# A chunk's decay table made on the chip, eight early load buffers, idle matmuls in the opening, a new order

## The chip, the cores and the metric

One core of one Trainium2 chip runs the whole program. The metric is device time in microseconds (us); the kernel before takes 593.6 us, the median of three runs (593.54 to 593.75). The engines are TensorE (PE; PEld is its weight load), VectorE (DVE), ScalarE (ACT), GpSimd (POOL) and SyncE (SP), which here issues all the DMAs.

## The reference, cut to what matters

```python
gamma = 1.0 - 2.0 ** (-5.0 - np.arange(H))               # retention: B=2, H=8, S=768, D=64
for t in range(S):
    state = gamma * state + k[:, :, t] (outer) v[:, :, t]
    y[:, :, t] = scale * q[:, :, t] @ state
x = y as 1536 tokens x 512
h = x @ w_in                                             # first MLP, 512 -> 2048 -> 512
P = a[0] + a[1]*h + a[2]*h**2 + a[3]*h**3
Q = 1.0 + abs(b[0])*abs(h) + abs(b[1])*h**2
x = (P / (Q + 1e-06)) @ w_out
h = x @ w2_in                                            # second MLP, same sizes
return (h / (1 + exp(-h))) @ w2_out
```

The weights arrive as 64-bit floats, and the kernel turns them into 32-bit ones on the chip.

## The kernel before, in words

The retention is cut into 12 chunks of 128 tokens (6 positions, 2 batches; chunk c is position c // 2). A chunk is a few small fp32 matmul blocks on PE: **scores** (line 435, from kT and qT), **within** (line 480, masked scores times vn), from the second position on **carried** (line 490, qT times the state bd), and until the last position **grow** (line 468, the state's growth from vn and kn). DVE multiplies the scores by the table msk (am, and in two chunks the buffers u and w), which holds, for each head, scale * gamma**(t - s) where t >= s and 0 elsewhere. POOL multiplies qT by the table gq, and kn is scaled by cst, on ACT for the first four chunks and on POOL after that. ACT and DVE take a chunk's result apart into a high part xh and a low part xl; ACT or DVE carry the growth into bd.

Both MLPs run in steps: group of 512 tokens by tile of 128 hidden features, 48 steps for each MLP. A step is 12 matmuls into h0 or h1 (line 526: high by high, low by high, high by low, over four input tiles), the activation on ACT and DVE, a split into gh and gl, and 12 matmuls into four accumulator banks (line 576). In the first 17 steps the activation's intermediate r lies in the h bank itself, so that step s + 2 can't start before the activation of step s is done with it. Weights come in units of 512 columns through three buffers raw and five wt, are converted by two ACT and two DVE instructions, and split into high (ACT) and low (POOL or DVE). Weights that are needed again are spilled to DRAM and loaded again.

The order of every engine is written out: ORDER is a packed list of places of all operations, made outside the program, and each engine runs its own operations in that order. SP's queue is in order too; a DMA takes one of eight completion semaphores in turn, so that it waits for the eighth DMA before it, and for whatever still reads its buffer. kT has two buffers, and qT, kn and vn have three each. The first four chunks (512 tokens) have to be done before step 0; the kernel runs 11 matmuls on zeros ahead of everything (line 644).

Of the kernel before, what the change touches and what calls it, by code (L numbers as in the profile page):

```python
# [18 lines left out]
P = 128  # L19
# [4 lines left out]
R = {'lw': -463.92, 'T0': 689.59, 'tau0': 13.93, 'tau1': 122.19, 'c0': -129.63, 'dc': 67.51, 'conv': 39.61, 'half': 427.29, 'absl': -34.77, 'raw': 455.03, 'ret': 752.06, 'spl': -417.39, 'hi': 301.24, 'lo': 31.56, 'inn': -277.93, 'later': -32.81, 'split': -554.53, 'out': 359.39, 'evac': -363.13, 'qload': -20.08, 'scl': 238.79, 'sc': 858.37, 'am': -44.15, 'gr': 112.48, 'av': -547.62, 'bd': 198.47, 'xh': -201.14, 'xl': 110.32, 'glp': 25, 'lop1': 15, 'lop2': 30, 'scp': 0, 'ps': 17, 'ksc': 103.89, 'qa': -467.29, 'ka': 4, 'late': 20, 'mid': 4, 'pev': -317.29, 'pld': -385.01, 'cg': -489.85, 'wm': 11, 'mk': 26.43, 'ck': 21.3, 'g2': (1, 0, 2), 'ch0': 269.21, 'ch1': -102.81, 'ch2': 64.3, 'ch3': 22.33, 'ch4': -52.46, 'ch5': 5.42, 'ch6': -78.23, 'ch7': 237.84, 'ch8': 90.06, 'ch9': -61.88, 'ch10': -106.39, 'ch11': -212.52, 'ru0': 218.22, 'lu0': -107.8, 'ru1': 40.68, 'lu1': -106.06, 'ru2': 91.09, 'lu2': 146.01, 'ru3': -37.17, 'lu3': -39.51, 'rhalf': 125.38}  # L24
# [30 lines left out]
    'c`q^bk%ZF65?aG)c>O40^ofMkY#Kp7NoM^ly|k0I(%#xZr)mrBtFbhWevycpUAM_oIVq>)gv`_FI!$A1T>UD2G>691`1(z9=>m<U{q(uy)&v?^',
    'b813esQq<@M$trCQcLM#{V6ZxyF8Q9I#8Et4?V6+bdcuJa#}|7YGR$K`E;3<)#aK*SLj-ut@*WrCe=AwURP>#{UK2`nhw@qGDO#DMIECtbiJ<D',
    'WLiKAY9Xzpvvhzi(sO!3PwIIstV4B!Zq&+JMT_WIt*V>#f?n0+nnF|QR!ym=bevYx(|S=aX$dW=#kH6=(CS)C>*_uorq}ekUe+^uLx<~4y`x`s',
    'm2T2Cx<$|G6|Jpxw4T=2@!C+gX$_sAjdZ`>)4MuSzw370q2Kh6-q#1ZQ-A1B9i@|Wv_96!`cEI~U%jQj^ofdvvfWx!N9X|sd!rL|ilRN$M|xX-',
    '>p?YB3vFS{EwHe5NE6#LO=?Ljgps|~aQ0l2S#o=)Y<qOC?$Tp=SdZvyeW6D+qJ_6qmeC?uNK0)gEVI4WH1<K$S}gmhuk?$))J&Gc(peTuZ;>pk',
    'MYbrG&0<>|i)s}ugQc{}mdh$xPOD*`wWigw{1(GvS_%84RjjJzwmjC%>RWazV0o>Y#kJa2#|m0Jt84wOkTtM|*4$cHNvm%8te!Qp##Y!$SxakW',  # L60
    '(JYZAwCL8>5?FjIZryBvm9{1}&|2Fd8*WXljkUA(HrUG8NE=~8ZIq3+VK&~T+eRy56|ATgvvM}UCRzs@Yu#;}b+kz~*?QPc8)HLkip{qbR^B>W',
    'S1W5>tfy_Z8Meu$+DuzuyKR?kv1zu|PTE47WxZ^+?XkVq$@*DuTV(rfuAR11w$irSVmn|vY@VI5v$o3m*b?h&%WbJGvx|1i_Sr$J>vOESZ?kh&',
    '%g@_tTVogOl5Mc{w$9etWqWN`?2z5I!*;~3+8w)V_w0?mwWD_3uGts6X*cY+eYG0?&Q91jtLg8phaa;B-qj!3U%PKl?S=ib$M(_OAJ|KKX5X#0',
    '|1j`6{=q(5HxIn0qmzg5PZr*P*-!gze~dk(*Yk!R!6SNo@8zMqk#~1<^%yQ5(<6Ck590|vtiQ6}9yWMlp@M!M*%NtUkL9sFsz>v1p30+p6wmB&',
    'Jhi9sw4TJ1dKORTSv{`D^Z1^?lY2@p>UlhcXYy>G*Ry**Pv#jsx99Y7p3&2LG4JpBy|@?f@?OIGcm*%%xx9!M@*G~;3wuFt<E6Z!SMtVQ#mjmb',
    'ujXyNiMR8nKG55HGw<Ndy|q{Ns@~E^`Dkz9t-Pam_D<f#2l-$h<3oI`kMq7hz=!&5ALb){gpc>BzQl+79G~m+e5ud(Wxm#zd+1=D&+tjU&4VCB',
    'Fu_;&dY|mme5P;r4ZheH`VQadi+q8v@-@EN_xlz<;hTM>@ALz{%Mbb?Kk4Cu!yZ03<za%5LDFElPxL9CE|}%dEkf|nQU@u5y}s4=_$EK*`~0Y1',
    '^wWOH&-i)Y?YI20KlbB(#Bci*zv_29S@6Uo26z3OpY<F5#xMAFzvegnsV5Ka`7?j(?>tSAGI;OlgRg$yANfQ7=g<Aa|NVXK5B!C{^jH4PF^Cj=',
    'cM5)Z+8|Z%(>aJ7#0frol;Deh^0-0NAYSm-Ke`9M{I_Qe{&@T#S`a-*5M&B62N?nhas?X14q^l`0}B!cv4SK);vi9wJIE5`39<$`f}BC#AYYIz',
    'C>rDsvIixCLP4>hcu*iH7?cc31%-nm!GFweCBF',  # L70
# [60 lines left out]
def retention_two_mlps(  # L131
# [104 lines left out]
    def at_chunk(c):  # L236
        return R[f"ch{c}"] + (5.5 * c if c < CPG else T0 + R["c0"] + R["dc"] * (c - CPG))
# [11 lines left out]
    class Parted:  # L249


        def __init__(self, name):
            self.t = cpool.tile([P, KD, GT], F32R, tag=name, name=name)
            self.cells = [[Cell() for _ in range(CPG)] for _ in range(KD)]
            self.all = [c for r in self.cells for c in r]
            self.chunk = [[r[o] for r in self.cells] for o in range(CPG)]

    xh = [Parted(f"xh{g}") for g in range(NG)]
    xl = [Parted(f"xl{g}") for g in range(NG)]

# [34 lines left out]
    kns, vns = Turns("kn", 3, [P, H, D], F32, at), Turns("vn", 3, [P, H, D], F32, at)  # L295
    qTs, kTs = Turns("qT", 3, [P, HP, P], F32, at), Turns("kT", 2, [P, HP, P], F32, at)
# [102 lines left out]
    shared = {}  # L399

    def attention(c, s_banks, o_banks):
# [5 lines left out]
        def load(n, turns, src):  # L407
# [4 lines left out]
        kT, qT = load(0.0, kTs, kt[b, ci]), load(0.1, qTs, qt[b, ci])  # L412
        vn = load(0.3, vns, v[b, ci])
        kn = load(0.4, kns, k[b, ci]) if grows else None
# [26 lines left out]
        for j in range(2):  # L441
            tt(
                "dve",
                rank + R["am"],
                heads(am[j].t),
                heads(sb_[j].t),
                msk.t[:, j, :, :],
                ALU.mult,
                [sb_[j], msk],
                [am[j]],  # L450
                port=False,
            )
# [284 lines left out]
```

## Time and profile before

| | |
|---|---|
| median of three runs | 593.6 us |
| the profiled execution: time, span | 591.33 us, 589.5 us |
| PE, share of the span busy | 97% |
| DVE, ACT, POOL | 71%, 67%, 23% |
| first matmul of step 0 | 27.58 us |
| first matmul of step 2 | 47.65 us |
| last matmul | starts at 584.96 us |

The span runs from the first to the last instruction. Matmuls are pipelined: one of 512 columns is shown with 0.39 us, but they start some 0.23 us apart, so a block's length is read from the chain of waits, where its parts follow each other. An fp32 matmul shows as two records. The granted clock is 1.00 for TensorE's 2.4 GHz and 0.50 for 1.2 GHz.

### The profile page before, as it was taken

The numbers are of one execution on the slowest core, as the hardware profiler recorded it, in microseconds if no ns is written. First come the engines' busy times: TensorE is split into PE (matmuls) and PEld (weight loads), VectorE is DVE, ScalarE is ACT, GpSimd is POOL, SyncE is SP. The second block draws the span as 40 slices with busy tenths as digits, with TensorE's granted clock in tenths as the row PEclk, the third lists the DMA queues.
The fourth block names the chain that finished last, engine by engine and source line by source line (L and its number), as shares of the span: only waits on it lengthen the run. The fifth ranks groups of instructions, "written<-read, shape, count | busy, mean of one in ns | idle before, by whom it ended". The sixth has DMA issues, their size and how long they took to land.

```text
span 589.5 us, 8100 instructions
## 1 busy us (share of the span) xinstructions
PE 574.0 (97%) x2950; PEld 474.0 (80%) x2950; DVE 417.5 (71%) x646; ACT 394.2 (67%) x690; POOL 132.9 (23%) x104
## 2 busy tenths in 40 slices
PE   6969999999999999999999999999999999999997
PEld 5858787888888888888888888878888888888885
DVE  2899999999899999999999977765332213233320
ACT  7887788999999887787999887764522312424212
POOL 0554674464435200000114364300000000000000
PEclk9998999999999999999999999999999999999999
DMA  8996855543122201302226565462320000130001
GB/s 327 339 370 239 303 192 162 180 125 117 62 81 81 73 1 36 126 18 91 76 68 214 179 212 152 156 217 84 108 89 1 1 1 18 54 123 3 0 1 72
DMA packets 33368, 70.02 MB, mean 119 GB/s; under 512 B 3632, under 2 KB 3632, under 8 KB 33328
## 3 DMA queue, kind: packets, MB, share of 16 engines
q1 hardware_dynamic: 33328, 69.51, 35.1%
q8 instruction: 23, 0.38, 0.3%
q14 instruction: 17, 0.14, 0.1%
HBM read 56.91 MB, written 12.58 MB: 118 GB/s over the span
## 4 chain that ended last, share of the span: by engine, by line
PE 91%; DMA 4%; DVE 2%; ACT 1%; issue 1%; SPq 0%; ACTq 0%
PE acc L576 43%; PE h L526 43%; DMA kT<-in_kt_dram 2%; PE a L490 2%; PE a L435 2%; PE a L480 1%; DVE wt L324 1%; DMA raw<-in_moe_w_out_dram 1%; DMA qT<-in_qt_dram 1%; PE a L468 1%; SPq L343 0%; ACT raw L309 0%; DVE am L317 0%; DVE w L324 0%; PE h L468 0%
## 5 line engine op out<-in xcount | busy, mean ns | idle before, releaser
L526 PE MATMUL h<-xh,ih 128*128 128x512 f32 x384 | 150.2, 391 | 0.1
L526 PE MATMUL h<-xh,il 128*128 128x512 f32 x384 | 149.5, 389 | 0.0
L526 PE MATMUL h<-xl,ih 128*128 128x512 f32 x384 | 149.4, 389 | 0.0
L324 DVE SCALAR_TENSOR_TENSOR w<-w,h 128x512 f32<-128x512 f32 x48 | 32.6, 684 | 78.4 <-ACT w L309 78.2
L526 PEld LDWEIGHTS h<-xh,ih 128*128 128x128 f32 x384 | 72.1, 188 | 16.1 <-DVE s L324 0.6
L526 PEld LDWEIGHTS h<-xh,il 128*128 128x128 f32 x384 | 72.1, 188 | 15.0
L526 PEld LDWEIGHTS h<-xl,ih 128*128 128x128 f32 x384 | 72.1, 188 | 14.8
L309 ACT ACTIVATE w<-h 128x512 f32<-128x512 f32 x48 | 28.1, 593 | 78.7 <-PE h L526 74.2
L576 PE MATMUL acc<-gh,oh 128*128 128x512 f32 x192 | 75.9, 395 | 0.0
L576 PE MATMUL acc<-gh,ol 128*128 128x512 f32 x192 | 74.8, 390 | 0.0
L576 PE MATMUL acc<-gl,oh 128*128 128x512 f32 x192 | 74.8, 390 | 0.0
L576 PE MATMUL acc<-oh,gh 128*128 128x512 f32 x192 | 74.7, 389 | 0.0
L576 PE MATMUL acc<-ol,gh 128*128 128x512 f32 x192 | 74.7, 389 | 0.0
L576 PE MATMUL acc<-oh,gl 128*128 128x512 f32 x192 | 74.7, 389 | 0.0
L317 DVE TENSOR_TENSOR gl<-w,gh 128x512 fp32r<-128x512 f32 x48 | 34.0, 715 | 44.1 <-ACT gh L309 44.1
L391 POOL TENSOR_TENSOR ol<-wt,oh 128x512 fp32r<-128x512 f32 x28 | 38.6, 1389 | 105.6 <-ACT oh L386 94.4
L309 ACT ACTIVATE gh<-w 128x512 fp32r<-128x512 f32 x48 | 29.8, 629 | 46.7 <-PE acc L576 31.6
L324 DVE SCALAR_TENSOR_TENSOR wt<-wt,raw 128x512 int32<-128x512 int32 x64 | 45.0, 707 | 12.0 <-ACT raw L309 7.2
L391 POOL TENSOR_TENSOR il<-wt,ih 128x512 fp32r<-128x512 f32 x28 | 39.5, 1419 | 51.3 <-ACT ih L386 34.2
L309 ACT ACTIVATE raw<-raw,par 128x512 int32<-128x512 uint32 x64 | 48.1, 758 | 1.5 <-DMA raw<-in_moe_w_in_dram 0.8
L324 DVE SCALAR_TENSOR_TENSOR s<-s,par,h 128x512 f32<-128x512 f32 x65 | 48.2, 744 | 1.0
L317 POOL TENSOR_TENSOR gl<-s,gh 128x512 fp32r<-128x512 f32 x26 | 35.2, 1353 | 59.4 <-ACT gh L309 37.7
(88 smaller groups left out, 960.2 us busy)
## 6 DMA issues: line engine op xcount, KB each, us to landing
raw<-in_moe_w_out_dram SPq DMA_DIRECT2D x32, 512.0 KB, 3.7
raw<-in_moe_w_in_dram SPq DMA_DIRECT2D x32, 512.0 KB, 4.6
spill<-wt SPq DMA_DIRECT2D x32, 256.0 KB, 4.6
wt<-spill SPq DMA_DIRECT2D x32, 256.0 KB, 3.0
qT<-in_qt_dram SPq DMA_DIRECT2D x12, 256.0 KB, 5.7
kT<-in_kt_dram SPq DMA_DIRECT2D x12, 256.0 KB, 5.7
vn<-in_v_dram SPq DMA_DIRECT2D x12, 256.0 KB, 6.0
kn<-in_k_dram SPq DMA_DIRECT2D x10, 256.0 KB, 5.6
```

What stands on the lines that cost most here:

```text
L309: lambda: nc.scalar.activation(out=out_, in_=in_, func=func, **kw),
L317: op(eng, dur, rank, lambda: e.tensor_tensor(out=out_, in0=in0, in1=in1, op=alu), reads, writes, port)
L324: lambda: nc.vector.scalar_tensor_tensor(out=out_, in0=in0, scalar=scalar, in1=in1, op0=op0, op1=op1),
L391: e.tensor_tensor(out=sl.t[nm + "l"][:, us], in0=wt.t, in1=sl.t[nm + "h"][:, us].bitcast(F32), op=ALU.subtract)
L435: nc.tensor.matmul(heads(sb_[j].t)[:, hp, :], kT.t[js, hp, :], qT.t[js, hp, :], start=True, stop=True)
L468: nc.tensor.matmul(st.t[j * D : (j + 1) * D, hp * D : (hp + 1) * D], kn.t[:, 2 * hp + j, :], vn.t[:, 2 * hp + j, :], start=(hp == 0), stop ...
L480: nc.tensor.matmul(heads(xo.t)[j * D : (j + 1) * D, hp, :], vn.t[:, 2 * hp + j, :], heads(am[j].t)[:, hp, :], start=(hp == 0), stop=not mo ...
L490: nc.tensor.matmul(heads(xo.t)[:, hp, :], old.t[:, hp, :], qT.t[:, hp, :], start=False, stop=True, skip_group_check=True,)
L526: nc.tensor.matmul(h.t, sl.t[w][:, ws], x[g].t[:, c, :], start=(n == 0), stop=(n == 3 * KD - 1))
L576: nc.tensor.matmul(a.t, a1, a2, start=(first and n == 0), stop=(last and n == 2))
```

## The change

1. msk (512 KB) is no longer loaded. POOL makes a causal table of ones, DVE a selector of one row for each half of the partitions; PE spreads the first row of the table decays[0] over all partitions by two fp32 matmuls of 512 columns, and DVE multiplies by a column of cst and the ones, eight instructions of 128x128.
2. kT and vn of chunks 2 to 5 get buffers of their own (256 KB each), in the memory that xh and xl of the last group take later. vn's turning buffers fall from three to two, qT's rise from three to four.
3. Eleven times three matmuls of 128 columns on zeros (33) are put among the opening's matmuls; the first matmul of step 0 stands behind all of them. They write columns 256 to 383 of bank h0, whose first 256 columns take the growth.
4. The planner's constants change, and ORDER with them. Among the constants: kn is scaled on POOL in all ten chunks (`ka` 0), 22 low parts gl are made on POOL instead of 26 (`glp`), 48 low parts of weights on each of POOL and DVE instead of 56 and 40 (`lop1`, `lop2`), the two late weight slots come in at use 16 instead of 20 (`late`), and 18 instead of 17 steps keep r in the bank (`ps`).

On PE, at the program's head, stood in the kernel before (h is h0 or h1; a, acc are accumulator banks):

```order
L644 MATMUL h_156<-u_0_132 128x128 x11
L435 MATMUL a_149<-qT_168,kT_171 128x128
L435 MATMUL a_150<-qT_168,kT_171 128x128
...
L435 MATMUL acc_151<-qT_169,kT_172 128x128
L435 MATMUL acc_152<-qT_169,kT_172 128x128
...
L480 MATMUL h_156<-am_175,vn_165 64x128
L480 MATMUL h_156<-am_176,vn_165 64x128
...
L468 MATMUL h_155<-vn_165,kn_162 64x64 x8
```

and now there stands (line 707 is the spreading, line 732 the matmuls without use, lines 448, 494 and 482 are scores, within and grow):

```order
L672 MATMUL h_154<-warm 128x128 x11
L707 MATMUL acc_152<-gq_182,s_0_134 128x512
L707 MATMUL acc_151<-gq_182,s_0_134 128x512
L732 MATMUL h_153<-warm 128x128 x6
L448 MATMUL a_147<-qT_165,kT_169 128x128
...
L732 MATMUL h_153<-warm 128x128 x6
L448 MATMUL acc_151<-qT_167,kT_c_174 128x128
...
L494 MATMUL h_154<-am_184,vn_163 64x128
...
L732 MATMUL h_153<-warm 128x128 x3
L482 MATMUL h_153<-vn_163,kn_160 64x64 x8
L732 MATMUL h_153<-warm 128x128 x3
```

Two spreading matmuls and 18 of the 33 on zeros now stand ahead of the scores of chunk 1, which come third; the other 15 follow in five threes, the last ahead of the scores of chunk 4. In both kernels chunks 0 to 4 stand ahead of step 0; only the growth of chunk 4 stood behind step 0, and now stands ahead of it. Behind step 1, before: scores, within, carried and grow of chunk 5, then scores, grow, within and carried of chunk 6, then step 2. Now: the same four blocks of chunk 5, then step 2, and chunk 6 spread over the steps behind it.

On DVE, from the first activation's multiplication by h to the instruction that gives its h bank free, stood before (u, s, t: activation; h as a target is r in the bank; wt: weights; am, xl, bd: chunks 5 and 6):

```order
L317 TENSOR_TENSOR s_0_136<-s_0_136,h_155 128x512
L324 SCALAR_TENSOR_TENSOR s_0_136<-s_0_136,par,h_155 128x512
L324 SCALAR_TENSOR_TENSOR s_1_137<-s_1_137,par,h_156 128x512
L317 TENSOR_TENSOR bd_161<-a_149,bd_161 64x4x64
L317 TENSOR_TENSOR xl_70<-a_150,xh_67 128x4x128
...
L324 SCALAR_TENSOR_TENSOR t_141<-u_0_132,h_155 128x512
...
L317 TENSOR_TENSOR am_175<-a_149,msk 128x512
L317 TENSOR_TENSOR am_176<-a_150,msk 128x512
L324 SCALAR_TENSOR_TENSOR h_155<-t_141,h_155 128x512
L324 SCALAR_TENSOR_TENSOR s_0_136<-s_0_136,par,h_155 128x512
```

and now:

```order
L329 TENSOR_TENSOR s_0_134<-s_0_134,h_153 128x512
L336 SCALAR_TENSOR_TENSOR u_0_130<-w_132,par,h_153 128x512
L336 SCALAR_TENSOR_TENSOR s_0_134<-s_0_134,par,h_153 128x512
L329 TENSOR_TENSOR am_185<-a_148,msk 128x512
L329 TENSOR_TENSOR am_184<-a_147,msk 128x512
L336 SCALAR_TENSOR_TENSOR u_1_131<-w_133,par,h_154 128x512
L329 TENSOR_TENSOR s_1_135<-s_1_135,h_154 128x512
L336 SCALAR_TENSOR_TENSOR t_139<-u_0_130,h_153 128x512
L336 SCALAR_TENSOR_TENSOR s_1_135<-s_1_135,par,h_154 128x512
L336 SCALAR_TENSOR_TENSOR h_153<-t_139,h_153 128x512
L336 SCALAR_TENSOR_TENSOR wt_127<-wt_127,raw_123 128x512
L336 SCALAR_TENSOR_TENSOR s_0_134<-s_0_134,par,h_153 128x512
```

These are twelve instructions in a row, with nothing left out between them. The am here belong to chunk 5, where before they were those of chunk 6, and what belongs to chunk 6 stands further down.

The diff, cut (of R and ORDER one line each way; the scores' reads and two evacuations only change form):

```diff
-R = {..., 'glp': 25, 'lop1': 15, 'lop2': 30, ..., 'ps': 17, ..., 'ka': 4, 'late': 20, ..., 'wm': 11, ...}
+R = {..., 'glp': 21, 'lop1': 19, 'lop2': 28, ..., 'ps': 18, ..., 'ka': 0, 'late': 16, ..., 'wm': 11, ...,
+     'fill': 11, 'fl': 41.18, 'lent': (('kT', 2), ('kT', 3), ('vn', 2), ('vn', 3), ('kT', 4), ('vn', 4), ('kT', 5), ('vn', 5))}
...
-    kns, vns = Turns("kn", 3, ...), Turns("vn", 3, ...)
-    qTs, kTs = Turns("qT", 3, ...), Turns("kT", 2, ...)
+    kns, vns = Turns("kn", 3, ...), Turns("vn", 2, ...)
+    qTs, kTs = Turns("qT", 4, ...), Turns("kT", 2, ...)
+    fpool = first_stack.enter_context(tc.tile_pool(name="first", bufs=1, side="right", reuse_waits="tile"))
+    lent = {(n, c): Buf(f"{n}_c{c}", ..., F32, fpool) for n, c in R["lent"]}
...
-            buf = turns()
+            buf = lent.get((name, c)) or turns()
...
-        op("pe", 2.72, now - R["inn"], mm_in, win + xh[g].all + xl[g].all, [h])
+        op("pe", 2.72, now - R["inn"], mm_in, win + xh[g].all + xl[g].all, [h] + [fill] * (s == 0))
...
-    dma(R["mk"], 1.32, msk.t[:].rearrange("p j a t -> p (j a t)"), consts[:, NGAM:], [], [msk])
+    dma(R["mk"], 0.66, shared[1].t[:].rearrange("p a x -> p (a x)"), decays[0], [], [shared[1]])
+    ...                                     # memsets of ones and pick, affine_select on ones
+        def spread(j=j, b_=b_):
+            nc.tensor.matmul(b_.t, pick.t[:, j * P : (j + 1) * P], shared[1].t[:].rearrange(...), start=True, stop=True)
+        for a in range(HP):
+            nc.vector.scalar_tensor_tensor(out=msk.t[:, j, a, :], in0=heads(b_.t)[:, a, :],
+                scalar=gk[:, 1, 2 * a + j : 2 * a + j + 1], in1=ones.t[:, 0:P], op0=ALU.mult, op1=ALU.mult)
...
-    warm = ew["u2"].bufs[0]
+    warm = Buf("warm", [P, P])
...
+    def filling():
+        for _ in range(3):
+            nc.tensor.matmul(bank["h0"].t[:, 2 * P : 3 * P], warm.t[:, 0:P], warm.t[:, 0:P], start=True, stop=True)
+    for n in range(R["fill"]):
+        op("pe", 0.65, R["fl"] + 1.5 * n, filling, [warm], [fill])
...
+        if c == (NG - 1) * CPG:             # before chunk 8: the lent buffers go, xh and xl of the last group come
+            op("host", 0.0, 0.0, make_way, [], [*lent.values(), *xh[NG - 1].all, *xl[NG - 1].all])
```

## Rows read from the trace of the kernel before

**Rows 1.** The page: the chain that ended last, by engine.

```profile
PE 91%; DMA 4%; DVE 2%; ACT 1%; issue 1%; SPq 0%; ACTq 0%
```

**Rows 2.** Busy time by stretch: length, engines, granted clock, DMA share, GB/s.

```profile
0.00:27.58 27.58, 20.79 (x270) 19.02 (x270) 15.24 (x28) 21.01 (x54) 8.99 (x12) 1.00 0.93 337
27.58:47.65 20.07, 15.64 (x154) 12.87 (x153) 18.18 (x30) 15.38 (x27) 9.82 (x8) 0.91 0.97 351
47.65:585.30 537.65, 537.53 (x2531) 442.09 (x2529) 384.10 (x589) 357.18 (x608) 114.13 (x84) 1.00 0.30 99
585.30:589.50 4.20, 0.05 (x1) 0.00 (x0) 0.00 (x0) 0.60 (x2) 0.00 (x0) 1.00 0.39 147
50.00:345.00 295.00, 295.00 (x1462) 241.78 (x1462) 284.35 (x438) 260.24 (x440) 97.75 (x73) 1.00 0.37 121
```

**Rows 3.** Waits of PE: line, releaser, us in total, times, longest.

```profile
PE acc L435 <- DMA kT<-in_kt_dram: 1.8, 1, 1.8
PE a L435 <- DVE bd L317: 1.6, 1, 1.6
PE h L480 <- DVE am L317: 1.6, 1, 1.6
PE a L468 <- DVE am L317: 1.5, 1, 1.5
PE a L480 <- DVE am L317: 1.4, 1, 1.4
PE a L435 <- DMA kT<-in_kt_dram: 0.8, 1, 0.8
```

**Rows 4.** The chain in order of time, end of the opening: start, us, what.

```profile
21.45 1.16 PE a L435 x16
22.61 0.62 PE h L468 x16
23.23 0.88 PE h L480 x16
24.10 1.09 PE h L490 x8
...
27.77 2.84 PE h L526 x12
```

**Rows 5.** The warming matmuls in the timeline: start, us, two records a matmul.

```profile
1.45 5.03 PE L644 MATMUL h<-u 128*128 128x128 f32 x22 [1.45 <-DVE par L648]
```

**Rows 6.** The chain ahead of step 2.

```profile
39.50 0.42 DVE bd L317
...
43.66 0.98 PE a L468 x16
44.64 1.71 PE a L480 x16
46.35 1.55 PE a L490 x8
```

**Rows 7.** The stretch of these three blocks, columns as in rows 2.

```profile
44.00:47.00 3.00, 3.00 (x31) 2.67 (x30) 2.76 (x5) 1.28 (x3) 1.38 (x2) 0.50 0.98 369
```

**Rows 8.** DVE at work without a gap, in order of time.

```profile
272.24 0.68 DVE L317 TENSOR_TENSOR s<-s,h 128x512 f32<-128x512 f32 x1
272.83 0.68 DVE L324 SCALAR_TENSOR_TENSOR r<-t,r 128x512 f32<-128x512 f32 x1
273.44 0.74 DVE L324 SCALAR_TENSOR_TENSOR s<-s,par,h 128x512 f32<-128x512 f32 x1
274.09 0.68 DVE L317 TENSOR_TENSOR s<-s,h 128x512 f32<-128x512 f32 x1
```

**Rows 9.** ACT behind step 0, in order of time.

```profile
31.93 0.77 ACT L309 ACTIVATE s<-h,par 128x512 f32<-128x512 f32 x1
32.60 0.68 ACT L309 ACTIVATE w<-h,par 128x512 f32<-128x512 f32 x1
```

More of the change, by code (lines that the diff above doesn't have):

```diff
@@ L256, in __init__, with make @@
             self.chunk = [[r[o] for r in self.cells] for o in range(CPG)]
+        def make(self, pool=cpool):
+            self.t = pool.tile([P, KD, GT], F32R, tag=self.name, name=self.name)
     xh = [Parted(f"xh{g}") for g in range(NG)]
     xl = [Parted(f"xl{g}") for g in range(NG)]
+    for g in range(NG - 1):
+        xh[g].make()
+        xl[g].make()
     class Slot:
@@ L399, in retention_two_mlps @@
     shared = {}
+    mcs = [Cell() for _ in range(2)]
     def attention(c, s_banks, o_banks):
@@ L405, in attention, with load @@
         more, grows = ci > 0, ci < NCI - 1
[L407 to L408 removed]
+        def load(n, turns, src, name=None):
+            buf = lent.get((name, c)) or turns()
             dma(rank - R["qload"] + n, 0.66, buf.t[:].rearrange("p a x -> p (a x)"), src, [], [buf])
             return buf
[L412 to L414 removed]
+        kT, qT = load(0.0, kTs, kt[b, ci], "kT"), load(0.1, qTs, qt[b, ci], "qT")
+        vn = load(0.3, vns, v[b, ci], "vn")
+        kn = load(0.4, kns, k[b, ci], "kn") if grows else None
         if grows:
@@ L448, in attention @@
                 ALU.mult,
-                [sb_[j], msk],
+                [sb_[j], mcs[j]],
                 [am[j]],
@@ L455, in attention @@
         if more:
-            gq = shared[ci] if ci in shared else load(0.5, gqs, decays[ci - 1])
-            shared[ci] = gq
+            if ci not in shared:
+                shared[ci] = load(0.5, gqs, decays[ci - 1])
+            gq = shared[ci]
             eng = "dve" if c < R["scp"] else "pool"
@@ L510, in attention, with high, low @@
         cols = slice(o * P, (o + 1) * P)
-        hi, lo = xh[g].t[:, :, cols], xl[g].t[:, :, cols]
-        act(rank + R["xh"], hi, heads(xo.t), AF.Copy, [xo], xh[g].chunk[o], True)
-        tt("dve", rank + R["xl"], lo, heads(xo.t), hi.bitcast(F32), ALU.subtract, [xo, *xh[g].chunk[o]], xl[g].chunk[o], port=False)
+        def high():
+            nc.scalar.activation(out=xh[g].t[:, :, cols], in_=heads(xo.t), func=AF.Copy)
+        def low():
+            hi = xh[g].t[:, :, cols].bitcast(F32)
+            nc.vector.tensor_tensor(out=xl[g].t[:, :, cols], in0=heads(xo.t), in1=hi, op=ALU.subtract)
+        op("act", 0.48, rank + R["xh"], high, [xo], xh[g].chunk[o])
+        op("dve", 0.6, rank + R["xl"], low, [xo, *xh[g].chunk[o]], xl[g].chunk[o])
+    fill = Cell()
     def step(s, l, g, u, j, first, last, part):
@@ L601, in step, with high, low @@
             elif last and l == 0:
-                hi, lo = xh[g].t[:, m, :], xl[g].t[:, m, :]
-                act(now + R["evac"], hi, a.t, AF.Copy, [a], xh[g].cells[m], True)
-                tt("dve", now + R["evac"], lo, a.t, hi.bitcast(F32), ALU.subtract, [a, *xh[g].cells[m]], xl[g].cells[m], port=False)
+                def high(m=m, a=a):
+                    nc.scalar.activation(out=xh[g].t[:, m, :], in_=a.t, func=AF.Copy)
+                def low(m=m, a=a):
+                    hi = xh[g].t[:, m, :].bitcast(F32)
+                    nc.vector.tensor_tensor(out=xl[g].t[:, m, :], in0=a.t, in1=hi, op=ALU.subtract)
+                op("act", 0.48, now + R["evac"], high, [a], xh[g].cells[m])
+                op("dve", 0.6, now + R["evac"], low, [a, *xh[g].cells[m]], xl[g].cells[m])
             elif last:
@@ L644, in warming @@
             nc.tensor.matmul(bank["h1"].t[:, 0:P], warm.t[:, 0:P], warm.t[:, 0:P], start=True, stop=True)
-    op("pe", 0.43 * R["wm"], -50.0, warming, [warm], [bank["h1"]])
+    op("pe", 0.21 * R["wm"], -50.0, warming, [warm], [bank["h1"]])
     op("dve", 0.1, -50.0, lambda: nc.vector.memset(cq, QD), [], [cqc])
@@ L651, in retention_two_mlps @@
     act(-50.0, warm.t[:, 0:1], warm.t[:, 0:1], AF.Abs_reciprocal_sqrt, [cqc], [warm], n=1, more=1.3, bias=cq)
+    shared[1] = gqs()
+    dma(R["mk"], 0.66, shared[1].t[:].rearrange("p a x -> p (a x)"), decays[0], [], [shared[1]])
+    pick, ones = ew["s1"].bufs[0], ew["s1"].bufs[1]
+    op("dve", 0.3, -49.0, lambda: nc.vector.memset(ones.t[:, 0:P], 1.0), [], [ones])
+    op("dve", 0.54, -49.0, lambda: nc.vector.memset(pick.t[:, 0 : 2 * P], 0.0), [], [pick])
+    for j in range(2):
+        row = slice(j * D, j * D + 1)
+        op("dve", 0.2, -49.0, lambda row=row, j=j: nc.vector.memset(pick.t[row, j * P : (j + 1) * P], 1.0), [], [pick])
@@ new lines, in causal @@
+    def causal():
+        nc.gpsimd.affine_select(
+            out=ones.t[:, 0:P],
+            in_=ones.t[:, 0:P],
+            compare_op=ALU.is_ge,
+            fill=0.0,
+            base=0,
+            pattern=[[1, P]],
+            channel_multiplier=-1,
+        )
+    op("pool", 0.5, -49.0, causal, [], [ones], True)
+    for j in range(2):
+        b_ = bank[f"acc{2 + j}"]
+        def spread(j=j, b_=b_):
+            nc.tensor.matmul(
+                b_.t, pick.t[:, j * P : (j + 1) * P], shared[1].t[:].rearrange("p a x -> p (a x)"), start=True, stop=True
+            )
+        op("pe", 0.88, R["mk"], spread, [pick, shared[1]], [b_])
+        for a in range(HP):
+            op(
+                "dve",
+                0.27,
+                R["mk"],
+                lambda j=j, a=a, b_=b_: nc.vector.scalar_tensor_tensor(
+                    out=msk.t[:, j, a, :],
+                    in0=heads(b_.t)[:, a, :],
+                    scalar=gk[:, 1, 2 * a + j : 2 * a + j + 1],
+                    in1=ones.t[:, 0:P],
+                    op0=ALU.mult,
+                    op1=ALU.mult,
+                ),
+                [b_, cst, ones],
+                [mcs[j]],
+            )
```

100 lines of the change are left out of this document (54 added, 46 removed).

## The prediction

> **What bounds the kernel now.** I read the page's chain first: PE makes up 91% of it [rows 1], so the question is where PE does anything but the steps' matmuls. The busy time by stretch answers that [rows 2]. From the first matmul of step 2 (47.65 us) to the last one PE is busy for 537.53 of 537.65 us at clock 1.00: nothing can be won there by shorter waits, and every us by which step 2 starts earlier or later is a us of the span. Two stretches stand ahead of it: the opening, 27.58 us with 20.79 busy (6.8 idle), and 20.07 us with 15.64 busy (4.4 idle) and a mean clock of 0.91. Behind the last matmul lie 4.2 us of evacuation and output, which keep their form. The waits [rows 3] show who makes PE idle: in the opening kT's loads (1.8 and 0.8 us), since its two buffers come free only with the scores, and the masked scores (1.6), which wait for the load of msk; behind step 0 the state's addition on DVE (1.6) and the masked scores (1.5 and 1.4). The blocks of a chunk cost PE, in the chain [rows 4]: scores 1.16, grow 0.62, within 0.88, carried 1.09. The warming takes 5.03 us for 11 matmuls, 0.457 each [rows 5]; the carried block's matmuls, of the same shape and type, take 1.09 / 4 = 0.272 [rows 4].
>
> **The opening, part by part.** What goes: the load of msk with its wait (1.6), and kT's waits (2.6). What comes stands in PE's own queue, so the sum is made of PE's work. Begin: 1.45 us now, the memset ahead of it shrinks from 512 columns to 128; I take 1.2. Warming: 5.0, as now. Two spreading matmuls: the trace has no fp32 one of 512 columns. From below a step's matmul, 2.84 / 12 = 0.24 [rows 4], from above four times the warming's 0.457, 1.8; nearest in kind are the chunk blocks, where 128 columns take 0.88 / 4 = 0.22 (within, two half-width matmuls side by side) to 0.272, so 0.9 to 1.1; I take 1.0 each, 2.0. The 33 matmuls on zeros: 0.22 to 0.272 by the same two blocks, from above 0.457; 7.3 to 9.0 (15.1 at the warming's rate). I take 8.2. The chunks' own blocks ahead of step 0: five scores, five within, three carried, and now five grows (four before): 5.8 + 4.4 + 3.3 + 3.1 = 16.6. One new wait: the three on zeros behind the first grow write the bank that the growth is read from, and stand behind that reading by ACT, two instructions of 64x256, some 0.4 each by the same shape on DVE [rows 6]; PE's whole queue stands behind it: 0.8, between 0 (if PE is late anyway) and 1.6. The sum: 1.2 + 5.0 + 2.0 + 8.2 + 16.6 + 0.8 = 33.8 us to step 0. Now it is 27.77, with one grow less; 28.4 like for like. So the opening is 5.4 us longer, if nothing of the 33 lies where PE would have waited. The bounds: 1.0 + 5.0 + 1.7 + 7.3 + 16.2 = 31.2 and 35.5.
>
> Does other work end later still? DMA: through kn of chunk 4, the last load that step 0 now stands behind, SP issues 22 loads of 256 KB and 5 of 512 KB, 8.4 MB; at the opening's 337 GB/s [rows 2] that is 25 us, before PE gets there. So the loads don't set the end. DVE: eight instructions of 128x128 for the table. 512 columns take 0.6 to 0.65 from start to start [rows 8], 256 columns 0.42 as a duration [rows 6]; so 0.25 to 0.6 each, I take 0.3. Six stand ahead of the first am: they run beside the first six on zeros and the first scores (8.2 to about 11), and the last two and the second am end near 12.3, when PE has just come to the within block. Cover is enough; at 0.6 each PE would wait 2 us more. POOL takes over four kn (now ACT's) and makes the ones: between the loads at 20 to 27 us and the grows it has room, and the last kn ends just ahead of its grow. I cost both at nothing, up to 1 us if POOL is late.
>
> **From step 0 to step 2.** Two steps of 12 matmuls: 2.84 + 2.72, 5.6 us; scores of chunk 5: 6.8. The within block waits for both am, 0.6 each and their latency, so until 8.1: a wait of 1.3, as now (1.4). Then within, carried and grow, 2.6, until 10.7. Step 2 needs bank h0 back. Step 0 ends 3.0 us after it began; ACT's first reading takes 0.77 [rows 9]; then DVE has twelve instructions in a row to the last reader of h0. Three fit ahead of the scores' end, nine follow from 6.8 on: 0.6 or 0.65 each [rows 8], 5.6, so 12.4. Step 2 starts 12.4 us after step 0, and PE idles 1.7 more. Bounds: 10.8 if DVE is ahead, 14.4 if three more conversions must be waited for. What stood ahead of step 2 and now stands behind it is the whole of chunk 6: scores, grow, within, carried, 3.75, and three changes of kind of matmul; 12 matmuls behind such a change take 2.84 against 2.72, so some 0.15 each: 4.2. Its scores wait 0.4 for the state's additions and xl, which DVE does last.
>
> The clock: the last three blocks ahead of step 2 take 0.98, 1.71 and 1.55 us [rows 6] instead of 0.62, 0.88 and 1.09 [rows 4], 1.65 more, at a granted clock of 0.50, that is 1.2 GHz [rows 7], after the 4.4 us of idle in the stretch. I take this as gone, since less idle is left (3.4); if it stays, 1.65 come on top. In the opening the clock is 1.00 through 6.8 us of idle [rows 2], so matmuls on zeros have nothing to keep up there. The Trainium skill (TensorE: Matmul & The Clock Gate, Part 1: The HAM clock gate) says that the half clock is the default, that activity lifts it and idle time brings it back; the warming's 0.457 us against 0.272 later agree with it, the opening's 1.00 through its waits does not. By this rule the matmuls on zeros would have their use in the opening, which no row shows, and the idle behind step 1, where none of them stands, would bring 0.50 again: 1.65 us more.
>
> **The sum.** New: 33.8 + 12.4 + 4.2 + 0.4 = 50.8 us at the place where the old kernel, by the chain, has 46.35 + 1.55 = 47.9 [rows 6]: 2.9 us longer. Behind it PE is full in both, and the same steps follow. The profiled execution took 591.33 us, 589.5 span and 1.8 around it; it becomes 594.2. The median of the three timed runs lies 2.3 us above it, so 593.6 becomes 596.5.
>
> **The rivals.** (A) The matmuls on zeros stand where PE waits anyway, and cost nothing: then the opening is bounded by the data. The last kn lands at 25 us, is scaled in 1.0 or so and grown in 0.62, with step 0 near 28.0: 28.0 + 12.4 + 4.6 = 45.0, 2.9 less than now, 590.7: faster. For it: the old opening has 6.8 us of idle [rows 2]. Against it: two thirds of these waits are what the change takes away. It decides if step 0 starts before 31 us. (B) DVE becomes the bound in the first MLP. It is busy for 284.35 of 295 us there [rows 2]. Four more low parts gl come to it (26 to 22 on POOL), 4 x 0.6 = 2.4; the eight weights' low parts fall in the second MLP. If the 10.6 us of idle can't take them, steps slip by 2.4: 598.9. Against it: xl, am and table leave DVE room while PE is late. (C) The change gives back what it takes: step 0 comes at its lower bound, 31.2 + 12.4 + 4.6 = 48.2 against 47.9, 593.9, no change that can be told. For it: the spreading, the 33 and the wait for ACT may all be at their low ends. Against it: they have to be so together. (D) The half clock comes again behind step 1, in the 3.4 us of idle that are left there: 596.5 + 1.65, 598.2. For it: the old stretch fell to 0.50 after 4.4 us of idle [rows 2, 7]. Against it: step 2 now lies between the two waits and is dense. This is how the page named above would have it.
>
> **How the numbers follow.** The forecast, slower by 2.9, gets 0.42, with 594.5 to 598.8 as its own range; A 0.20, C 0.15, B 0.12, D 0.11. A measurement of this kernel can tell about 0.2% (1.2 us) from no change. Faster: 0.17 of A, and 0.02 each of C and of the forecast: 0.21. Same: 0.02 of A, 0.11 of C, 0.05 of the forecast: 0.18. Slower: 0.61. The range goes down into A, to 591.0, which leaves out some 0.1, and up past B and D together with the upper bounds of the opening, to 600.0.
>
> **What would show it.** In the new profile: step 0's first matmul near 33.8 us; PE busy nearly throughout from 1.2 us to it, with the 33 at 0.22 to 0.27 us each and no wait for kT, msk or DMA at all; a wait of 1.3 for am behind step 1 and one of 1.7 for DVE ahead of step 2; PE full from there. I am wrong if step 0 starts before 31 us, if PE waits for data behind groups on zeros, or if PE idles behind step 4, where the old one did not.

## The result: 0.9% slower, and the profile after

The changed kernel takes 598.68 us (median of 6 runs, 597.92 to 599.79) against 593.57 of the kernel before (6 runs): a ratio of 1.0093, 95% interval 1.0069 to 1.0118. Forecast were 596.5, slower; the direction held, and the loss is 5.1 us instead of 2.9. The profiled execution took 598.64, with a span of 596.9 against 589.5, so 7.4 longer; why the medians lie closer together is taken up behind the experiments.

First the busy time by stretch, cut as in [rows 2]: opening, step 0 to step 2, step 2 to about the last matmul, the output, and the first MLP. Columns: PE, PEld, DVE, ACT, POOL busy, granted clock, DMA share, GB/s.

```profile
0.00:35.14 35.14, 32.87 (x356) 28.46 (x357) 22.23 (x44) 14.18 (x26) 15.88 (x18) 1.00 0.87 290
35.14:47.83 12.69, 9.70 (x85) 7.80 (x81) 12.26 (x21) 12.24 (x23) 7.05 (x6) 1.00 0.97 354
47.83:592.00 544.17, 544.08 (x2582) 445.06 (x2583) 393.36 (x607) 361.76 (x610) 97.47 (x73) 1.00 0.31 99
592.50:596.90 4.40, 0.28 (x2) 0.00 (x0) 0.00 (x0) 0.84 (x2) 0.00 (x0) 1.00 0.43 161
50.00:345.00 295.00, 294.91 (x1492) 240.18 (x1491) 282.11 (x441) 257.03 (x431) 87.26 (x67) 1.00 0.37 120
```

PE is busy for 32.87 of the opening's 35.14 us, where 6.8 of 27.58 were idle before; the stretch at clock 0.91 is gone; behind step 2 PE is full, as it was. The list of PE's waits in the first 60 us is short (columns as in [rows 3]):

```profile
PE a L494 <- DVE am L329: 1.4, 1, 1.4
PE h L549 <- DVE s L336: 1.2, 1, 1.2
PE h L672 <- DVE warm L668: 1.1, 1, 1.1
PE h L732 <- ACT bd L321: 0.9, 1, 0.9
PE a L482 <- POOL kn L329: 0.4, 1, 0.4
PE h L494 <- DVE xl L531: 0.2, 1, 0.2
```

No load is in this list: kT and the masked scores of the opening, which stood there in [rows 3], are gone. The timeline of PE in the opening, which answers to [rows 4, 5] (start, us, two records a matmul for these shapes; the us of a row run to the last modelled end, so a cost is read from start to start):

```profile
1.12 5.06 PE L672 MATMUL h<-warm 128*128 128x128 f32 x22 [1.12 <-DVE warm L668]
5.97 2.12 PE L707 MATMUL acc<-gq,s 128*128 128x512 f32 x4
7.93 1.50 PE L732 MATMUL h<-warm 128*128 128x128 f32 x12
9.36 1.16 PE L448 MATMUL a<-qT,kT 64*128 64x128 f32 x16
10.45 1.60 PE L732 MATMUL h<-warm 128*128 128x128 f32 x12
11.99 1.16 PE L448 MATMUL acc<-qT,kT_c 64*128 64x128 f32 x16
...
20.49 0.94 PE L732 MATMUL h<-warm 128*128 128x128 f32 x6
21.36 0.32 PE L494 MATMUL h<-u,vn 128*64 128x128 f32 x1
```

The matmuls on zeros (L732) take 1.43 and 1.54 us for the two groups of six, and 0.87 for three: with seven such threes 9.04 us in all, 0.274 each.

Both kernels have 2304 matmuls of the steps (h and acc), with the steps in the same sequence, and both timelines can be counted through. The first of them starts 7.56 us later than before, the 25th (step 2; chunk 6 is still to come in the new order) 0.18, the 601st and the 701st, when all chunks are done in both, 4.2, the 1101st and the 1301st 6.1, the 1501st and the 1701st 5.7, the last 7.4. So 4.2 us of the 7.4 are the opening and the new order of the chunks, 0.4 comes back in the second MLP, and 3.6 lie in two stretches, between the 741st and the 1101st (1.9) and behind the 1701st (1.7): there the last group of rows (g = 2) goes through the first and the second MLP. Nothing was expected there.

In the chain, a step's 12 matmuls on x (h) and those on gh and gl (acc) behind them take 2.72 us per 12 in the kernel before, from one end to the other:

```profile
238.10 2.04 PE acc L576 x9
240.14 2.72 PE h L526 x12
242.86 5.44 PE acc L576 x24
248.30 5.44 PE h L526 x24
```

The same stretch after the change, in the last group of rows (g = 2) of the first MLP:

```profile
253.64 2.08 PE acc L599 x9
255.72 2.81 PE h L549 x12
258.53 2.76 PE acc L599 x12
```

2.81 instead of 2.72 for h, and for acc 0.04 a block too much, whether it has 9 or 12 matmuls: 2.08 against 2.04, 2.76 against 2.72. The granted clock is 1.00 in both. In the groups before it, and in the first two of the second MLP, the pace is the old one (2.72); in the last group of the second MLP it is 5.61 for 24 again. 32 h blocks with 0.09 and 25 stretches of acc with 0.04 would be 3.9 us, for the 3.6 counted.

### The profile page after: what moved, and what is told of

It is laid out like the page before. It is cut to its first block, busy times and chain, and to the rows that moved or that the text cites. A ratio compares the mean times of both kernels' runs of the same rounds, so it can differ in the third digit from the quotient of the medians.

```text
span 596.9 us, 8209 instructions
## 1 busy us (share of the span) xinstructions
PE 587.4 (98%) x3020; PEld 481.6 (81%) x3020; DVE 427.9 (72%) x670; ACT 389.4 (65%) x657; POOL 120.4 (20%) x97
## 4 chain that ended last, share of the span: by engine, by line
PE 97%; DVE 2%; ACT 1%; issue 0%; ACTq 0%
PE acc L599 44%; PE h L549 44%; PE a L448 2%; PE h L732 1%; PE a L504 1%; PE a L494 1%; PE h L672 1%; PE h L494 1%; PE a L482 1%; PE acc L448 0%; DVE wt L336 0%; PE acc L707 0%; PE h L482 0%; DVE h L336 0%; DVE am L329 0%
## 5 line engine op out<-in xcount | busy, mean ns | idle before, releaser
L403 POOL TENSOR_TENSOR il<-wt,ih 128x512 fp32r<-128x512 f32 x24 | 33.0, 1379 | 137.5 <-ACT ih L398 137.4
L336 DVE SCALAR_TENSOR_TENSOR wt<-wt,raw 128x512 int32<-128x512 int32 x64 | 47.6, 749 | 5.6 <-ACT wt L321 2.8
L321 ACT ACTIVATE wt<-raw 128x512 f32<-128x512 f32 x64 | 42.6, 668 | 10.1 <-DMA raw<-in_moe_w_in_dram 8.1
L336 DVE SCALAR_TENSOR_TENSOR wt<-raw,wt 128x512 int32<-128x512 int32 x64 | 47.7, 748 | 0.6
L321 ACT ACTIVATE s<-h,par 128x512 f32<-128x512 f32 x48 | 37.1, 774 | 12.3 <-PE h L549 4.6
```

The lines of the kernel that those rows point to most:

```text
L321: lambda: nc.scalar.activation(out=out_, in_=in_, func=func, **kw),
L336: lambda: nc.vector.scalar_tensor_tensor(out=out_, in0=in0, scalar=scalar, in1=in1, op0=op0, op1=op1),
L403: e.tensor_tensor(out=sl.t[nm + "l"][:, us], in0=wt.t, in1=sl.t[nm + "h"][:, us].bitcast(F32), op=ALU.subtract)
```

## The experiments

**What the last group has of its own.** Only its x was moved: xh2 and xl2 now lie at the upper end of the on-chip memory, where the lent buffers were. The compiled programs tell at which byte of a partition each tile starts. Modulo 512, the weights, gh, gl and the x of all groups start at 384 in the kernel before; in the changed one xh2 (byte 212,960) and xl2 start at 480, all else at 384. That gave the first theory, that the place of an operand sets PE's pace; its rivals were the new order, and the far end of the memory as such. In what follows, the place of a tile is its first byte modulo 512.

**e1: 32 bytes on.** An unused tile behind the lent buffers, and one behind xl2:

```
+    fpool.tile([P, 8], F32, tag="pad1", name="pad1")
...
+                last.tile([P, 8], F32, tag="pad2", name="pad2")
```

> The changed kernel with 32 unused bytes per partition behind the eight lent buffers, and behind the last group's x that later stands there: xh2 then starts at byte 212,928 of a partition (a multiple of 64) instead of 212,960 (32 over one). Nothing else differs. Theory 1 (place of x): the last group's 384 matmuls that read x go from 0.2342 to 0.2267 us, and the time falls by 384 x 0.0075 = 2.9 us, to about 595.8. Theory 2 (the new order: more DVE and ACT traffic on those buffers while the last group runs): the interval stays 0.234 and the time 598.7. Theory 3 (the upper end of the memory is far from PE, whatever the byte): no change either, since the buffers move by 32 bytes only.

Measured: 597.21 us (6 runs), 1.0091 of the kernel before on the same chip (1.0068 to 1.0115); measured so, nothing is shown against the changed kernel's 1.0093, and the answer has to come from the trace. The chain of the same stretch:

```profile
252.72 2.09 PE acc L600 x9
254.81 2.75 PE h L550 x12
257.56 2.77 PE acc L600 x12
```

h went from 2.81 to 2.75 through 32 bytes, with the order unchanged and x still at the far end: the place matters. But it didn't go to 2.72, and acc stayed slow, so order and far end could still have the rest. A multiple of 64 bytes was not what it takes.

**e4: the kernel before, with the last x 32 bytes off.** The x of the first two groups stay where they were (384), xh2 and xl2 go to 416, and the allocator puts all that follows (weights, gh, gl) at 448:

```
-    xh = [Parted(f"xh{g}") for g in range(NG)]
-    xl = [Parted(f"xl{g}") for g in range(NG)]
+    xh = [Parted(f"xh{g}") for g in range(NG - 1)]
+    xl = [Parted(f"xl{g}") for g in range(NG - 1)]
+    cpool.tile([P, 8], F32, tag="pad1", name="pad1")
+    xh.append(Parted(f"xh{NG - 1}"))
+    xl.append(Parted(f"xl{NG - 1}"))
+    cpool.tile([P, 8], F32, tag="pad2", name="pad2")
```

> The kernel before, with nothing changed but the places: xh2 and xl2 start 32 bytes over a multiple of 64 (53,664 instead of 37,248, and 61,856), all else at multiples of 64. Theory 1 (place of x): its 384 matmuls on the last group's x go from 0.2267 to 0.2342 us, 593.6 + 2.9 = 596.5. Theories 2 and 3 (order; upper end of the memory): 593.6 as before, since the order is the old one and the buffers stay in the lower part.

Measured: 599.26 us, 1.0133 (1.0105 to 1.0162), 7.7 us and not 2.9. Every group is slow:

```profile
239.22 2.07 PE acc L580 x9
241.29 2.80 PE h L530 x12
244.09 5.46 PE acc L580 x24
249.55 5.60 PE h L530 x24
```

The expected mechanism at nearly three times the size, 96 steps of 0.08: the first two groups' x had not moved, but the weights had, by 64 bytes. So it isn't where x stands, but where it stands against something else that moved. And acc, whose two operands had moved together, is 5.46 for 24: 0.02 too much in all, at the start of the block behind h.

**e5: 96 bytes on.** As e1 with 24 elements for 8; xh2 and xl2 start at 384 modulo 512, like the weights.

> The changed kernel with 96 unused bytes behind the lent buffers and behind the last group's x: xh2 starts at byte 212,864, which leaves 384 over a multiple of 512, as the weights and the other groups' x do; 32 bytes on, at 212,928, it left 448, and in the changed kernel 480. Theory 1 (PE keeps its pace of 226.67 ns when the moving operand and the weights stand alike within 512 bytes): all matmuls of the last group, those on x and the ones behind them, go to 226.67 ns; against the changed kernel 32 blocks x 0.13 us = 4.1 us are gone, 598.7 - 4.1 = 594.6, and against the run with 32 bytes 2.7 us, 597.2 - 2.7 = 594.5. Theory 2 (what was left at 32 bytes comes from the new order): 229.5 to 230 ns as there, and 597.

Measured: 595.32 us (12 runs), 1.0039 (1.0009 to 1.0068). h and acc are back at the old pace (a single h block behind these rows still takes 2.77):

```profile
238.73 2.72 PE h L550 x12
241.45 2.72 PE acc L600 x12
244.17 2.72 PE h L550 x12
246.89 3.40 PE acc L600 x15
250.29 2.72 PE h L550 x12
253.01 2.05 PE acc L600 x9
```

In the medians, which come from different chips, 3.4 us of the 5.1 are gone by 96 bytes of nothing; against the kernel before on its own chip the loss falls from 0.93% to 0.39%, which is 3.2 us. The trace says it without the medians: counted as above, the steps' matmuls of e5 lose 0.1 us in the two stretches in which the changed kernel loses 3.6 (and e1's lose 2.2). So what was left in e1 is shown to be place too, neither order nor far end, both of which e5 keeps.

**e6: the kernel before, all 64 bytes on.** x, weights, gh and gl at 448; the weights stand where they stood in e4:

```
+    cpool.tile([P, 16], F32, tag="pad1", name="pad1")
     xh = [Parted(f"xh{g}") for g in range(NG)]
```

> The kernel before with 64 unused bytes ahead of the first x, so that all groups' x, the weights and gh and gl start 64 bytes later, all by the same. In the kernel before with only the last x at 32 bytes, weights and gh stood at these same places, x of the first two groups 64 bytes off them, and all groups were slow (233.5 ns, +7.7 us). Theory 1 (what counts is how x stands to the weights): no change, 226.67 ns everywhere and 591.6 us. Theory 2 (what counts is how each stands to a multiple of 128 bytes): slow in all groups, 597 to 600 us.

Measured: 592.21 us, 0.9982 (0.9950 to 1.0014), and 2.72 us for nearly every block of 12 (single ones in its chain take up to 2.9). What counts is the distance between x and what moved in e4, not the place of either.

**e11 and e12: which distance.** The kernel before, with 128 and then 256 bytes between the last x and the first weights:

```
     xl = [Parted(f"xl{g}") for g in range(NG)]
+    cpool.tile([P, 32], F32, tag="pad1", name="pad1")      # e12: [P, 64]
```

> The kernel before with 128 unused bytes between the last x and the first weights: all weights, gh and gl stand 128 bytes further from x than before, in all three groups. Theory 1 (a distance that is a multiple of 128 bytes keeps the pace): 226.67 ns and 592 us. Theory 2 (it takes a multiple of 512): all blocks on x slow, 230 to 234 ns, and 597 to 600 us.

> As the run before, with 256 bytes instead of 128 between the last x and the first weights, so that weights, gh and gl stand 256 bytes further from x than in the kernel before. Theory 1 (a multiple of 256 keeps the pace): 226.67 ns, 592 us. Theory 2 (it takes a multiple of 512): blocks on x at 230 to 234 ns, and 597 to 600 us, as with 128 bytes.

Measured: 598.86 us, 1.0118 (1.0074 to 1.0161), and 592.73 us, 0.9990 (0.9968 to 1.0013). The chain with 128 and with 256:

```profile
241.63 2.79 PE h L527 x12
244.42 5.45 PE acc L577 x24
```

```profile
241.23 2.04 PE acc L577 x9
243.27 2.72 PE h L527 x12
245.99 5.44 PE acc L577 x24
```

With all runs together (distance of x from the weights modulo 512, us for 12 matmuls on x): 0: 2.72 (before, e5, e6); 256: 2.72 (e12); 32 or 64 below: 2.80 (e4); 64 above: 2.75 (e1); 96 above: 2.81 (changed kernel); 128 below: 2.79 (e11). In e4, e11 and e12 the weights, gh, gl and all that follows them moved by the same; that the distance from the weights is the one that counts is argued from what the matmuls on x read, x and weights alone; no run moved the weights by themselves.

**e2: no matmuls on zeros.** The second question is the opening.

```
-        for _ in range(3):
+        for _ in range(0):
             nc.tensor.matmul(bank["h0"].t[:, 2 * P : 3 * P], warm.t[:, 0:P], ...)
```

> The changed kernel without the 33 matmuls on zeros; every other instruction stands in its order. Theory 1 (they cost what they take in PE's queue): 9.1 us of matmuls and the 0.9 us wait for ACT go out of the opening, and some 3 to 4 us of waits for loads and for DVE's am come in; step 0 near 29 instead of 35.1, the time 592 to 593. Theory 2 (they fill waits that are there anyway): step 0 stays at 34 to 35 and the time at 598. Theory 3 (they keep the clock up): step 0 comes earlier as in theory 1, but the granted clock is 0.50 somewhere in the opening or behind step 1, which gives back 1.7 to 5 us: 594 to 598.

Measured: 596.07 us, 1.0069 (1.0047 to 1.0091), 2.6 less than with them (1.4 by the ratios). Step 0 starts at 31.52 instead of 35.14. Of 9.04 us of matmuls and 0.9 of the wait for ACT, 3.6 come out of the opening; in place of the rest stand waits that the 33 had covered, of which PE's list has, among others:

```profile
PE h L494 <- DVE xl L531: 2.4, 2, 1.5
PE acc L448 <- DVE msk L717: 2.0, 1, 2.0
PE acc L448 <- DMA qT<-in_qt_dram: 1.5, 1, 1.5
PE a L448 <- DMA qT<-in_qt_dram: 0.2, 1, 0.2
```

So theories 1 and 2 are both partly right: some two thirds of the 33 lie inside waits, one third costs. And not all of the 3.6 us arrives: step 2 still starts 3.6 earlier, but from the 111th of the steps' matmuls on the lead is 2.4, since PE now waits ahead of a chunk's scores, at 69 us, for the state that DVE adds up. The changed kernel has no such wait there:

```profile
PE a L448 <- DVE bd L329: 1.2, 1, 1.2
```

So "every us by which step 2 starts earlier or later is a us of the span", as the prediction had it, doesn't hold here. Theory 3 doesn't show in this profile (clock 1.00 throughout the opening), but it does in the runs: the mean granted clock of an execution is 0.9997 over the 6 runs of the changed kernel and 0.9993 over e1's 6 on the chip of e2, and 0.9978 over the 6 without zeros.

**e3: both edits** (32 bytes, no zeros).

> Both edits at once: the 32 bytes of padding and no matmuls on zeros. If the two costs are independent the gains add: 2.9 and 6, so 598.7 - 8.9 = 589.8, below the kernel before (593.6). If the matmuls on zeros are hidden or hold the clock, 593 to 596; if the place of x has no effect, 592.5.

Measured: 594.86 us (11 runs), 1.0050 (1.0033 to 1.0067). In the medians e1 gave 1.5 and e2 2.6; together 3.8. In the profiled executions the last of the steps' matmuls starts 2.1 us earlier in e1 than in the changed kernel, 2.4 in e2 and 4.8 in e3. So they add, but to less than expected, since each was sized too large.

**e7: 96 bytes, no zeros.**

> The changed kernel with 96 bytes of padding and without the 33 matmuls on zeros. If the costs add: the run with 32 bytes and no zeros (594.9) less the 2.7 us that were left in the last group: 592.2, within 0.2% of the kernel before (591.6). If the order holds the last group back, 594.9 again.

Measured: 592.56 us (12 runs), 0.9993 (0.9967 to 1.0020), as expected: with place and zeros taken out, the change is worth nothing that can be told. In its profiled execution the half clock came in the opening, just behind PE's waits for loads:

```profile
PE h L495 <- DMA vn_c<-in_v_dram: 2.4, 1, 2.4
PE acc L449 <- DMA qT<-in_qt_dram: 1.1, 1, 1.1
```

```profile
23.50:26.80 3.30, 3.30 (x31) 2.96 (x32) 1.93 (x4) 3.23 (x7) 2.22 (x2) 0.50 1.04 334
```

PE is busy throughout that row at 0.50, the lower of its two levels (1.2 GHz). This is what the matmuls on zeros are good for: e5, the same kernel with them, on the same chip, has a mean granted clock of 0.9994 over its 12 runs, none below 0.999, and e7 0.9975, down to 0.992.

**e8: no warming either** (the loop of the warming at range(0), on top of e7).

> As the run before, and without the 11 warming matmuls too: PE has nothing to do until the decays' load has landed. Theory 1 (the opening is set by DVE, which can begin the table only when the spreading matmuls are through, and these stand behind 5.0 us of warming): step 0 some 3 us earlier than in the run with the warming (27 to 28 instead of 30.9), 589 to 590 us, below the kernel before. Theory 2 (warming lifts PE's clock): the blocks of the opening run at 1.2 GHz for some us; spreading and scores take twice as long, and nothing or less is gained: 592 to 594. Theory 3 (the loads set the end of the opening): step 0 stays near 30, 591.5 to 592.

Measured: 591.69 us (12 runs), 0.9981 (0.9954 to 1.0009). Step 0 starts at 31.41, and not at 27 to 28: theory 1 fell. The spreading begins at 3.73, when the decays have landed, but takes 3.69 us instead of 2.12, and the blocks at 10.55 and 12.51 fall into a stretch at 0.50:

```profile
3.73 3.69 PE L708 MATMUL acc<-gq,s 128*128 128x512 f32 x4 [3.73 <-DMA gq<-in_decays_dram]
7.35 1.16 PE L449 MATMUL a<-qT,kT 64*128 64x128 f32 x16
10.55 2.03 PE L449 MATMUL acc<-qT,kT_c 64*128 64x128 f32 x16 [2.04 <-DVE msk L718]
12.51 1.83 PE L495 MATMUL h<-am,vn 128*64 128x128 f32 x16
```

```profile
10.70:14.00 3.30, 3.30 (x30) 3.08 (x32) 1.63 (x2) 1.30 (x2) 2.31 (x3) 0.50 1.06 404
```

Theory 2 describes what happened. The warming's 5.0 us and what it saves are about even.

**e9: zeros only where PE waits** (96 bytes; of the eleven groups only four):

```
-        op("pe", 0.65, R["fl"] + 1.5 * n, filling, [warm], [fill])
+        op("pe", 0.65, R["fl"] + 1.5 * n, filling if n in (2, 3, 9, 10) else lambda: None, [warm], [fill])
```

> The changed kernel with 96 bytes of padding, and of its eleven groups of three matmuls on zeros only four: the two that stand where PE waits 2.0 us for DVE's reading of the spread banks, and the two ahead of the blocks that wait for xl. Theory 1 (matmuls on zeros cost nothing inside a wait and everything outside): step 0 as without any, 31 to 32 us, and the time at or below that of the run without zeros, 591.5 to 592.5. Theory 2 (they keep the clock up wherever they stand): the granted clock of the runs goes from a mean of 0.9975 without zeros to 0.999 or more, which is worth 0.6 us more: 591 to 592. Theory 3 (each costs its time): 12 x 0.28 = 3.3 us, and 595.

Measured: 592.14 us (12 runs), 0.9994 (0.9968 to 1.0020); step 0 at 31.25, mean granted clock 0.9993 over the 12 runs against 0.9975 over e7's 12, on another chip. The twelve matmuls cost nothing that shows, and with them the clock stays nearly as high as with the 33; the 0.4 us against e7 can't be told from nothing. Against e5, with the same place of x and all 33, the 601st of the steps' matmuls starts 3.8 us earlier in the profiled execution (0.3 behind the kernel before, where e5 is 4.1 behind), and the wait for DVE's state that e2 has does not come up: this is about what the other 21 and the wait for ACT cost, with 0.3 for the warming, which was through earlier in e9's execution.

**e10: as e9, with 6 warming matmuls.**

> As the run before, with 6 warming matmuls instead of 11, so that the spreading can begin when the decays have landed (3.7 us) and not at 6.0. Theory 1 (DVE sets the opening, and starts when the spreading is through): step 0 some 1 to 2 us earlier than in the run before, 590 to 591, under the kernel before. Theory 2 (the spreading then runs at the low clock, 3.7 us as without any warming): it ends near 7.4 instead of 8.3, 0.9 earlier, 591. Theory 3 (the loads set it): no change.

Measured: 591.61 us (12 runs), 0.9984 (0.9964 to 1.0005); step 0 at 32.15. The spreading starts at 3.84 and its first scores follow at 6.78 instead of 7.34 in e9, but then PE waits 1.65 us for qT's load: what is won ahead is lost to the loads, and in this execution the clock fell to 0.50 once more; the mean over the 12 runs is 0.9984. Against e9 nothing is shown. e8 and e10 have the lowest medians of all; both lie under the changed kernel by 7 us (1.1% by the ratios, some 6.5 us), and neither beats the kernel before beyond its interval.

## Why the prediction was right in direction and short in size

**The opening, right but 1.3 us short.** Begin and warming: 6.2 forecast, 5.97 measured. Spreading: 2.0 and 1.96 (5.97 to 7.93). Matmuls on zeros: 8.2 and 9.04; that is the mis-sized term, at the upper end that the prediction had from the carried block. Wait for ACT: 0.8 and 0.9. The chunks' blocks: 16.6 and 17.0 (what is left of 35.14 when 7.93, 9.04, 0.93 and 0.22 for xl are taken off). Step 0 to step 2: 12.4 and 12.69, with the wait for am at 1.4 (1.3 forecast), that for DVE at 1.2 (1.7), and 0.4 for POOL's kn, which was costed at nothing. Chunk 6 behind step 2: 4.6 and 4.0 (the lag of 4.2 behind it less the 0.18 at step 2); and the old place, read as a start like the new one, is 47.65 and not 47.9. 1.3 + 0.3 - 0.6 + 0.3: +4.2 where +2.9 was forecast.

**"Behind it PE is full in both, and the same steps follow": the step that failed.** PE is full and the steps are the same, but they don't run at the same pace. The move of xh2 and xl2 was taken as free. It puts the last group's x 96 bytes (modulo 512) off the weights and costs 3.6 us in the profile; in e5, with those bytes mended, 0.1 of them is left, and the median is 3.4 us lower.

**The step from the profile to the median failed too.** The prediction added 2.3 us, by which the old kernel's median lay above its profiled execution, to the new one as well. The new median lies on its profiled execution (598.68 and 598.64). Clock accounts for a difference of that size: on the chip of e5 to e8 the runs of the kernel before have a mean granted clock between 0.979 and 1.000, and the 12 of 35 below 0.992 took 594.9 us on average, the 6 at 0.999 or more 590.3; the changed kernel's six runs all have 0.999 or 1.000. That the 2.3 themselves are clock is argued, since the clock of the timed runs behind the 593.6 isn't on record. So the forecast's parts were off by +1.3 (opening and chunks), +3.6 (place of x), -0.4 (second MLP) and -2.3 (clock), and 596.5 became 598.7. That the median came within 2.2 us of the forecast is in part luck: in the profiled executions the loss is 7.3 us (598.64 against 591.33), two and a half times the 2.9, and the failed step to the median hid half of that error.

**The rivals.** A (the zeros are hidden) is two thirds true, by e2: what they take in PE's queue isn't what their removal gives back. B (DVE becomes the bound) didn't come: DVE is busy for 282.11 of 295 us, PE for 294.91. C's opening (31.2) lay lower than any seen with the 33 (34.22, in e1). D didn't come either: from 35.14 on the clock is 1.00.

**"Matmuls on zeros have nothing to keep up there": wrong.** One profiled execution with 1.00 through its idle time was taken for a rule. Without them some executions fall to 0.50 in the opening, as e7's did behind waits of 1.1 and 2.4 us. So do executions of the old order, which has none among its chunks either; these are e4's and e12's (columns as in [rows 2]):

```profile
8.00:11.00 3.00, 3.00 (x30) 2.78 (x29) 1.37 (x3) 2.77 (x8) 0.00 (x0) 0.50 1.04 397
15.80:19.00 3.20, 3.20 (x36) 3.08 (x38) 2.34 (x4) 1.59 (x3) 2.81 (x2) 0.50 1.05 387
```

The Trainium skill (TensorE: Matmul & The Clock Gate, Part 1: The HAM clock gate) has idle time bring the half clock back; e7 and e8 agree with it, and the forecast had set its use for the zeros aside.

**What stays open.** Why the distance counts: the runs show which distances are slow, not what in PE or the memory makes them so. Whether odd multiples of 256 hold everywhere (one was tried, in one kernel). And what sets the opening once the zeros are gone: PE waits for DVE in e3, and for DVE and loads in e2, e7 and e10; no run took either away.

## What to carry to other kernels

When a buffer moves, look at its start address before calling the move free: here x and the weights, read by the same matmuls, keep PE's full pace at a distance of 0 or 256 bytes modulo 512, and lose 1 to 3% at 32, 64, 96 or 128; a few unused bytes mend it. Cost filler on a full engine twice, by what it takes in the queue and by the waits that come back without it, and put it only into those waits. And compare kernels with their granted clock beside the time, over many runs: one profiled execution doesn't show which clock the next one gets.

## What the runs showed of the hardware that was not expected

- 12 of the steps' matmuls on x (128x512; their tiles are declared F32R in the kernel, and the timeline prints f32) take 2.72 us, 2.75, 2.79, 2.80 or 2.81, at a granted clock of 1.00, by the distance of x from the weights in the memory. The Trainium skill (SBUF — State Buffer, Operand start alignment) wants a start at a multiple of the element's size, 4 bytes here, and says that this is about what is legal and not about speed. All places tried keep to that, and their pace differs.
- The slow pace carries over: acc blocks whose own operands stand well lose 0.01 to 0.05 us in all behind a slow h block, 2.08 for 9 matmuls and 2.76 for 12, and then run at the full pace.
- With the 33 small matmuls the mean granted clock is 0.9993 to 0.9997 (changed kernel, e1, e5: 0.9997, 0.9993, 0.9994); without any it is 0.9974 to 0.9978 (e2, e3, e7). Twelve of them inside waits go with 0.9993 in e9, and with 0.9984 in e10, which has fewer warming matmuls.
- The spreading, fp32 with 512 columns, takes 0.98 us a matmul in the changed kernel (1.96 for two), 0.86 in e5 (1.72 for two, start to start) and 1.8 without warming ahead of it (e8, 3.62 for two), while the granted-clock column shows 1.00 for all three stretches. In the traces the first record of the clock comes at 6.44 us in the changed kernel, inside its spreading, at 5.70 in e5, just ahead of it, and at 7.23 in e8, near its end: the column doesn't tell the level ahead of its first record.
